# Linear attention and an MLP-mixer: how twenty-four units get the column maximum of k on all partitions

## The chip, the cores and the metric

One NeuronCore of a Trainium2 chip. Its engines are named as the profile names them: PE (TensorE matmuls; PEld are its weight loads), DVE (VectorE), ACT (ScalarE), POOL (GpSimd) and SP (SyncE, which here only issues loads). The metric is the device time of one execution in microseconds, the median of several runs. A profiled execution has a time of its own and a span, from the first to the last recorded instruction.

## The reference

```python
k_s = k - np.max(k, axis=2, keepdims=True)      # over the sequence, per (batch, head, column)
k_s = np.exp(k_s)
k_s = k_s / (np.sum(k_s, axis=2, keepdims=True) + 1e-09)
kv = np.einsum('bhsd,bhse->bhde', k_s, v)
attn = np.einsum('bhsd,bhde->bhse', q_s, kv)    # q_s: softmax of q over its 64 columns
# then, on x = attn as (batch, 576, 512):
h = np.maximum(x.transpose(0, 2, 1) @ w_tok1, 0.0) @ w_tok2
u = x + h.transpose(0, 2, 1)
out = u + np.maximum(u @ w_ch1, 0.0) @ w_ch2
```

q, k and v are float32 of shape (8, 8, 576, 64); the four weights are 64-bit (576x256, 256x576, 512x1536, 1536x512). The softmax of k runs over the sequence, so its maximum is one number for each of the 64 columns of a head.

## The kernel before, in words

**Units.** A unit is one batch and two heads, 32 in all (`NU`). The first eight (`NE`) are "early", the other twenty-four "late". A unit has k twice: `kt_t` with the columns of two heads on the 128 partitions and the sequence along the free dimension, where DVE takes the maximum in one reduction (`mc`, one number per partition, L219), and, for late units, `k_t` with the sequence on the partitions, which the later matmul (`stage_kv`, L277) needs. In `k_t` the maximum must be subtracted along the free dimension, so every partition needs all 128 numbers. Early units take the exponential in `kt_t` and transpose it on PE. A late unit does this: ACT scales an identity with `mc` into a diagonal `dg` (L233), PE multiplies an all-ones matrix with it (L235), which puts the row of 128 maxima on every partition, ACT copies it out of PSUM into `mb` (L236), POOL subtracts `mb` from `k_t` (L237), ACT takes the exponential (L238). `dg` and `mb` have one buffer each, `mc` two, `kt_t` one in the late units, `k_t` and `q_t` two.

**The rest of a unit.** `softmax_q` on DVE and ACT (with ten small exponentials, L251, in four units of each kind); q is split into a high and a low part (`qh` on ACT, `ql` on POOL, L114 and L115) and transposed in 32x32 blocks (L315, L323, `qth`, `qtl`). PE then makes `stage_kv`, `stage_y` (L337), `stage_h1` (L345) and `stage_u` (L381). The result `u` is split into `uh` and `ul` (L388, L389).

**The MLP.** The rows of the result are taken in nine groups of 512. For each group and each of twelve slices `f`, `ch1` makes 12 matmuls (L409), ACT and DVE make `h2h` and `h2l` of them (L412, L413), and `ch2` makes 12 more into four PSUM banks (L421). There are 108 such steps. Products run in float32r with high and low parts.

**Weights.** Each 64-bit weight tile is loaded into a staging buffer (`stg`, L166) and turned into float32 by DVE, ACT, and DVE again (L174 to L181; L181 is the last to read the buffer), and split into `cw` (L114 on ACT, L115 on DVE). Slices 4 to 11 are loaded during the first steps, the last of them through two staging buffers.

**What sets the order.** The kernel is written unit by unit and step by step; a scheduler then lists the instructions of each engine by its own estimates of durations. Each engine runs its list strictly in order, and SP issues its loads in order too, waiting ahead of each until the buffer is free. `soft(n + 1)`, which holds the lines above, is written right behind the first stage of unit n, `begin(n + 2)`, which loads a unit, half a step later.

Of the kernel before, what the change touches and what calls it, by code (L numbers as in the profile page):

```python
# [8 lines left out]
F32 = mybir.dt.float32  # L9
F32R = mybir.dt.float32r  # L10
U32 = mybir.dt.uint32
AF = mybir.ActivationFunctionType
# [3 lines left out]
P = 128  # L16
# [4 lines left out]
def attn_mixer_kernel(ctx: ExitStack, tc: tile.TileContext, q, k, kt, v, wt, out, dims):  # L21
# [3 lines left out]
    nc = tc.nc  # L25
# [10 lines left out]
    NE = 2 * NJ  # L36
# [13 lines left out]
    ident = const.tile([P, P], F32R, name="ident")  # L50
# [11 lines left out]
    ones = const.tile([P, P], F32, name="ones")  # L62
# [26 lines left out]
    dg = lay.tile([P, P], F32, name="dg")  # L89
    for i in range(3):  # L90
        slots[i][1] = lay.tile([P, NJ, CW], F32R, name=f"ul{i}")
    mb = lay.tile([P, P], F32, name="mb")
# [16 lines left out]
    def f32(ap):  # L109
        return ap.bitcast(F32)  # L110
# [8 lines left out]
    def ps_unit(dtype=F32):  # L119

        pools = unit_banks[0]
        pool, name = pools[turn[0] % len(pools)]
        turn[0] += 1
        return pool.tile([P, 512], dtype, name=name)
# [88 lines left out]

    turned_k = []

    def softmax_k(u):
        ktt = u["kt"]
        mc = sm.tile([P, 1], F32, name="mc")
        nc.vector.tensor_reduce(mc, ktt, axis=AX.X, op=ALU.max)  # L219
        kx = u["k"]  # L220
        if u["early"]:
            nc.vector.tensor_scalar(mc, mc, -1.0, None, op0=ALU.mult)
            nc.scalar.activation(ktt, ktt, AF.Exp, bias=mc)
            t = ps_unit()
            for c in range(C):
                nc.tensor.transpose(t[:, c * P : (c + 1) * P], ktt[:, c * P : (c + 1) * P], f32(ident))
            nc.scalar.copy(kx[:, 0:C, :], t.rearrange("p (c d) -> p c d", c=C))
            t = ps_unit()
            turned_k.append(nc.tensor.transpose(t[:, 0:P], ktt[:, S0 : S0 + P], f32(ident)).ins)
            nc.scalar.copy(kx[:, C, :], t[:, 0:P])  # L230
            return

        nc.scalar.activation(dg, f32(ident), AF.Copy, scale=mc)  # L233
        t = ps_unit()
        nc.tensor.matmul(t[:, 0:P], ones, dg, start=True, stop=True)  # L235
        nc.scalar.copy(mb, t[:, 0:P])  # L236
        nc.gpsimd.tensor_tensor(kx, kx, mb.unsqueeze(1).broadcast_to([P, C1, P]), op=ALU.subtract)  # L237
        nc.scalar.activation(kx, kx, AF.Exp)  # L238

# [223 lines left out]
    def soft(n):  # L463
        if n < NU:
            softmax_k(units[n])
            softmax_q(units[n])
# [194 lines left out]
```

## Time and profile before

| | |
|---|---|
| median of 3 runs | 822.23 us (821.69 to 822.65) |
| the profiled execution | 822.09 us, span 820.3 us, 11946 instructions |
| granted TensorE clock | 0.995 of full |
| moved by DMA | 63.55 MB, mean 77 GB/s |

The page of the profile lists the busy time of each engine, then the costliest groups of instructions by line. Matmuls are pipelined, so their busy times overlap and are no cost each; the distance between starts is. "Idle before, <-releaser" is the time that an engine waited ahead of an instruction and what ended that wait. The chain of waits goes back from the last instruction to what released it, step by step.

### The profile page before, as it was taken

What the parts mean: (1) busy time and instruction counts of PE and PEld (TensorE: products, weight loads), DVE (VectorE), ACT (ScalarE), POOL (GpSimd) and SP (SyncE); (2) the same over time, 40 slices, a digit from 0 to 9 for tenths busy, and PEclk for the clock granted to TensorE, in tenths of its full rate; (3) what the DMA queues carried; (4) which work ended last, traced back from release to release, by engine and by line L of the source; (5) the groups of instructions that cost most, each with busy time, mean ns of one, the idle gap of its engine ahead of it and who ended that gap; (6) DMA issues with size and microseconds to landing.
All of it is one profiled execution on the core that took longest, in us unless ns stands there. A gap on an engine that the chain in (4) does not pass through costs nothing.

```text
span 820.3 us, 11946 instructions
## 1 busy us (share of the span) xinstructions
PE 803.5 (98%) x4512; PEld 678.1 (83%) x4512; DVE 490.5 (60%) x1104; ACT 340.0 (41%) x898; POOL 84.4 (10%) x69
## 2 busy tenths in 40 slices
PE   7899999989999999999999999999999999999997
PEld 6688888878888888888888888888888888888886
DVE  6999998897875455855576555845575324113112
ACT  6976564457544344443434443434443421101110
POOL 1000010102201011111111111101111100000100
PEclk9999999999999999999999999999999999999999
DMA  9753433424222112312232221312121001001001
GB/s 298 241 161 93 150 108 113 139 83 126 64 73 85 48 53 63 109 52 64 64 114 63 64 64 35 113 47 63 39 91 48 15 1 51 1 1 51 1 1 51
DMA packets 60634, 63.55 MB, mean 77 GB/s; under 512 B 40865, under 2 KB 40993, under 8 KB 60577
## 3 DMA queue, kind: packets, MB, share of 16 engines
q1 hardware_dynamic: 55392, 53.36, 22.2%
q10 hardware_dynamic: 5184, 9.44, 3.1%
q8 instruction: 35, 0.57, 0.3%
q14 instruction: 23, 0.18, 0.1%
HBM read 53.35 MB, written 9.44 MB: 77 GB/s over the span
## 4 chain that ended last, share of the span: by engine, by line
PE 89%; DVE 6%; DMA 3%; ACT 1%; SPq 1%; issue 0%; DVEq 0%; ACTq 0%
PE ps_h L409 34%; PE ps_o L421 34%; PE ps_h L381 8%; PE ps_h L337 5%; PE ps_h L277 2%; DMA stg<-in_w 2%; PE ps_h L345 1%; DMA kt_t<-in_kt 1%; PE ps_o L381 1%; PE ps_h L235 1%; PE ps_o L337 1%; DVE mc L219 1%; DVE q_t L323 1%; DVE cv_s L176 1%; DVE cv_s L181 1%; DVE stg L179 0%
## 5 line engine op out<-in xcount | busy, mean ns | idle before, releaser
L409 PE MATMUL ps_h<-uh,cw 128*128 128x512 f32 x864 | 268.6, 391 | 0.3 <-DVE cw L115 0.3
L421 PE MATMUL ps_o<-h2h,cw 128*128 128x512 f32 x864 | 250.0, 392 | 2.2 <-DVE cw L115 2.2
L421 PEld LDWEIGHTS ps_o<-h2h,cw 128*128 128x128 f32 x864 | 160.0, 188 | 34.7 <-ACT h2h L412 2.4
L409 PEld LDWEIGHTS ps_h<-uh,cw 128*128 128x128 f32 x864 | 159.3, 188 | 31.6 <-DVE cw L115 0.8
L413 DVE SCALAR_TENSOR_TENSOR h2l<-ps_h,h2h 128x512 fp32r<-128x512 f32 x108 | 74.3, 688 | 170.4 <-ACT h2h L412 170.2
L412 ACT ACTIVATE h2h<-ps_h 128x512 fp32r<-128x512 f32 x108 | 64.4, 596 | 253.8 <-PE ps_h L409 251.5
L409 PE MATMUL ps_h<-ul,cw 128*128 128x512 f32 x432 | 168.7, 390 | 0.0
L421 PE MATMUL ps_o<-h2l,cw 128*128 128x512 f32 x432 | 151.9, 394 | 0.0
L409 PEld LDWEIGHTS ps_h<-ul,cw 128*128 128x128 f32 x432 | 81.1, 188 | 17.4
L421 PEld LDWEIGHTS ps_o<-h2l,cw 128*128 128x128 f32 x432 | 79.7, 188 | 15.9
L323 DVE COPY q_t<-cv_s 32x160 f32<-32x160 f32 (+1 forms) x264 | 62.1, 235 | 45.2 <-POOL ql L115 41.9
L237 POOL TENSOR_TENSOR k_t<-k_t,mb 128x640 f32<-128x640 f32 x24 | 38.0, 1583 | 350.6 <-ACT mb L236 350.6
L115 POOL TENSOR_TENSOR ql<-q_t,qh 128x640 fp32r<-128x640 f32 x24 | 39.2, 1633 | 220.7 <-ACT qh L114 218.2
L245 DVE TENSOR_REDUCE st<-q_t 128x10 f32<-128x640 f32 x32 | 26.2, 817 | 38.2 <-DMA q_t<-in_q 38.2
L323 ACT COPY q_t<-cv_s 32x128 f32<-32x128 f32 (+1 forms) x120 | 36.8, 307 | 2.1 <-DVE cv_s L315 0.7
L256 ACT ACTIVATE q_t<-q_t 128x640 f32<-128x640 f32 x24 | 17.7, 739 | 40.4 <-DVE q_t L255 40.4
L381 PE MATMUL ps_h<-w2h,hh 128*128 128x256 f32 (+1 forms) x112 | 32.6, 299 | 0.0
L381 PE MATMUL ps_h<-w2l,hh 128*128 128x256 f32 (+1 forms) x112 | 32.6, 296 | 0.0
L389 DVE TENSOR_TENSOR ul<-ps_h,uh 128x320 fp32r<-128x320 f32 (+4 forms) x76 | 26.8, 372 | 7.4 <-ACT uh L388 6.8
L388 ACT CAST uh<-ps_h 128x320 fp32r<-128x320 f32 (+4 forms) x76 | 24.4, 337 | 15.6 <-PE ps_h L381 11.2
L381 PE MATMUL ps_h<-w2h,hl 128*128 128x320 f32 (+1 forms) x112 | 29.8, 300 | 0.3 <-DVE hl L353 0.2
L219 DVE TENSOR_REDUCE mc<-kt_t 128x1 f32<-128x640 f32 x32 | 25.9, 809 | 4.8 <-DMA kt_t<-in_kt 3.5
(144 smaller groups left out, 1077.8 us busy)
## 6 DMA issues: line engine op xcount, KB each, us to landing
stg<-in_w SPq DMA_DIRECT2D x28, 512.0 KB, 4.0
kt_t<-in_kt SPq DMA_DIRECT2D x32, 320.0 KB, 3.2
q_t<-in_q SPq DMA_DIRECT2D x32, 320.0 KB, 3.1
v_t<-in_v SPq DMA_DIRECT2D x64, 128.0 KB, 2.6
out<-stg ACTq DMA_DIRECT2D x32, 256.0 KB, 2.1
k_t<-in_k SPq DMA_DIRECT2D x24, 320.0 KB, 3.3
v_t<-in_v SPq DMA_DIRECT2D x32, 32.0 KB, 2.5
out<-part ACTq DMA_DIRECT2D x4, 256.0 KB, 2.3
```

The costliest lines, as they stand in the source:

```text
L115: lo_eng.tensor_tensor(lo, src, f32(hi), op=ALU.subtract)
L219: nc.vector.tensor_reduce(mc, ktt, axis=AX.X, op=ALU.max)
L237: nc.gpsimd.tensor_tensor(kx, kx, mb.unsqueeze(1).broadcast_to([P, C1, P]), op=ALU.subtract)
L245: nc.vector.tensor_reduce(st[:, 0, :], qt, axis=AX.X, op=ALU.max)
L323: eng(qx[ys, 0:n, xs], turned[xs, 0:n, ys])
L337: nc.tensor.matmul(y[:, 0:TOK], a, w, start=(i == 0), stop=(i == len(mm) - 1))
L381: nc.tensor.matmul(t[:, 0:N], a, w, start=(i == 0), stop=(i == len(mm) - 1))
L389: nc.vector.tensor_tensor(ul, src, f32(uh), op=ALU.subtract).ins,
L409: nc.tensor.matmul(t, cw[f][x][:, n, :], w, start=(i == 0), stop=(i == 3 * NJ - 1))
L412: nc.scalar.activation(hh, t, AF.Relu).ins,
L413: nc.vector.scalar_tensor_tensor(hl, t, 0.0, f32(hh), op0=ALU.max, op1=ALU.subtract).ins,
L421: nc.tensor.matmul(o, cw[f][x][:, n, :], w, start=(first and i == 0), stop=(last and i == 2))
```

## The change

For the late units the diagonal, the product with the ones and the copy are not made. Instead SP writes the 128 numbers of `mc` into a row in memory (128 partitions of one number each into 128 numbers that lie together) and reads this row back into `mb`, the same row for each of the 128 partitions. A late unit has its own row, 24 in all. Nothing else is written differently; `dg` stays allocated.

```diff
+    THROUGH = NE
+    dram = ctx.enter_context(tc.tile_pool(name="dram", bufs=2, space=bass.MemoryType.DRAM))
 
     def softmax_k(u):
...
-        nc.scalar.activation(dg, f32(ident), AF.Copy, scale=mc)
-        t = ps_unit()
-        nc.tensor.matmul(t[:, 0:P], ones, dg, start=True, stop=True)
-        nc.scalar.copy(mb, t[:, 0:P])
+        if u["n"] < THROUGH:
+            nc.scalar.activation(dg, f32(ident), AF.Copy, scale=mc)
+            t = ps_unit()
+            nc.tensor.matmul(t[:, 0:P], ones, dg, start=True, stop=True)
+            nc.scalar.copy(mb, t[:, 0:P])
+        else:
+            row = dram.tile([1, P], F32, name="row")
+            nc.sync.dma_start(row.rearrange("o p -> p o"), mc)
+            nc.sync.dma_start(mb, row.broadcast_to([P, P]))
         nc.gpsimd.tensor_tensor(kx, kx, mb.unsqueeze(1).broadcast_to([P, C1, P]), op=ALU.subtract)
         nc.scalar.activation(kx, kx, AF.Exp)
```

`THROUGH` is 8, the number of early units, which return ahead of these lines; so no unit makes the product. Lines behind the change have numbers that are higher by 4 and then by 9.

The scheduler makes new lists of the instructions. Three places.

First, DVE in the loop that turns the last weights into float32. L174 is the first and L181 the last instruction that reads a staging buffer, L115 the split into `cw`, L413 (L422 in the changed kernel) makes `h2l`, and L219 (L223) is the maximum of k. Before:

```order
L177 TENSOR_SCALAR stg<-stg 128x512
L413 SCALAR_TENSOR_TENSOR h2l_112<-ps_h,h2h_108 128x512
L219 TENSOR_REDUCE mc<-kt_t 128x1
L179 SCALAR_TENSOR_TENSOR stg<-stg 128x512
L174 TENSOR_SCALAR cv_s<-stg 128x512
L181 TENSOR_TENSOR cv_s<-stg,cv_s 128x512
L176 SCALAR_TENSOR_TENSOR cv_s<-stg,cv_s 128x512
L115 TENSOR_TENSOR cw_1388<-cv_s,cw_1388 128x4x128
L177 TENSOR_SCALAR stg<-stg 128x512
```

The changed kernel, between the 13th and the 15th `h2l`:

```order
L181 TENSOR_TENSOR cv_s<-stg,cv_s 128x512
L223 TENSOR_REDUCE mc<-kt_t 128x1
L422 SCALAR_TENSOR_TENSOR h2l_113<-ps_h,h2h_109 128x512
L176 SCALAR_TENSOR_TENSOR cv_s<-stg,cv_s 128x512
L115 TENSOR_TENSOR cw_1390<-cv_s,cw_1390 128x4x128
L177 TENSOR_SCALAR stg<-stg 128x512
L174 TENSOR_SCALAR cv_s<-stg 128x512
L179 SCALAR_TENSOR_TENSOR stg<-stg 128x512
L223 TENSOR_REDUCE mc<-kt_t 128x1
L181 TENSOR_TENSOR cv_s<-stg,cv_s 128x512
L176 SCALAR_TENSOR_TENSOR cv_s<-stg,cv_s 128x512
```

Before, the maximum shown is the only one between the 11th `h2l` and the 29th L181; now there are five, two of them in the rows shown. Ahead of the next-to-last split of weights (the last tile that `ch1` needs) stand 21 maxima instead of 13, and by the 23rd `h2l` all 32 stand instead of 16. L174 and the next L181 are also further apart.

Second, PE where the second group's last step is due: the last matmuls of `stage_y` of the first late unit (L337, now L346) and what follows. L421 (L430) is `ch2`, L409 (L418) `ch1`, L345 (L354) is `stage_h1` and L381 (L390) `stage_u`. Before:

```order
L337 MATMUL ps_h<-w1tl,qh 128x256
L421 MATMUL ps_o<-h2h_109,cw_1388 128x512 x8
L421 MATMUL ps_o<-h2l_113,cw_1388 128x512 x4
L345 MATMUL ps_h<-kvf_110,ys 128x128 x2
L381 MATMUL ps_h<-qth,kvh 128x320
L381 MATMUL ps_h<-qtl,kvh 128x320
```

The changed kernel:

```order
L346 MATMUL ps_h<-w1tl,qh 128x256
L354 MATMUL ps_h<-kvf_110,ys 128x128 x2
L390 MATMUL ps_h<-qth,kvh 128x320
L418 MATMUL ps_h<-uh_100,cw_1095 128x512 x2
L418 MATMUL ps_h<-ul_104,cw_1095 128x512
L418 MATMUL ps_h<-uh_100,cw_1095 128x512 x2
```

The `ch2` group, which needs the last weights, moved behind `stage_h1`, a whole `ch1` group and half of `stage_u`. From the 23rd `ch1` group on, PE's order is the same as before but for the products.

Third, SP. Before, a late unit's loads:

```order
L137 DMA kt_t<-in_kt 128x640
L140 DMA q_t<-in_q 128x640
L154 DMA v_t<-in_v 128x4x64 x2
L155 DMA v_t<-in_v 64x2x64
L144 DMA k_t<-in_k 128x640
L137 DMA kt_t<-in_kt 128x640
```

The changed kernel, near the end of the weights loop (L244 writes a row, L245 reads it back):

```order
L244 DMA row<-mc 128x1
L137 DMA kt_t<-in_kt 128x640
L244 DMA row<-mc 128x1
L166 DMA stg<-in_w 128x1024
L137 DMA kt_t<-in_kt 128x640
L154 DMA v_t<-in_v 128x4x64 x2
L155 DMA v_t<-in_v 64x2x64
L144 DMA k_t<-in_k 128x640
```

and in a late unit:

```order
L245 DMA mb<-row 128x128
L140 DMA q_t<-in_q 128x640
L154 DMA v_t<-in_v 128x4x64 x2
L155 DMA v_t<-in_v 64x2x64
L144 DMA k_t<-in_k 128x640
L245 DMA mb<-row 128x128
```

The kt loads and the rows' writes moved out of the late units and stand between the weight loads (L166) and the first late units' loads, where each write waits for its maximum. In a late unit only the row's read is left, behind the load of k of the unit before.

## The prediction

> **What bounds the kernel now.** I read the page's totals first, then busy time by stretches, then the idle times of PE in the one stretch that has any, then the chain of waits there, and last the rows of the instructions that go. The page's totals, and the chain's shares:
>
> ```profile
> PE 803.5 (98%) x4512; PEld 678.1 (83%) x4512; DVE 490.5 (60%) x1104; ACT 340.0 (41%) x898; POOL 84.4 (10%) x69
> PE 89%; DVE 6%; DMA 3%; ACT 1%; SPq 1%; issue 0%; DVEq 0%; ACTq 0%
> ```
>
> Busy time by stretches (busy us per engine, granted clock, DMA share, GB/s):
>
> ```profile
> 100.00:120.00 20.00, 20.00 (x90) 16.56 (x89) 19.69 (x40) 14.06 (x53) 3.08 (x1) 1.00 0.34 113
> 120.00:140.00 20.00, 20.00 (x90) 16.54 (x89) 17.64 (x33) 7.29 (x12) 0.00 (x0) 1.00 0.32 105
> 140.00:160.00 20.00, 20.00 (x108) 16.40 (x106) 16.94 (x31) 8.47 (x16) 1.86 (x1) 1.00 0.43 131
> 160.00:180.00 20.00, 17.48 (x88) 14.55 (x87) 18.29 (x43) 10.22 (x26) 3.14 (x2) 1.00 0.23 69
> 180.00:200.00 20.00, 19.45 (x137) 16.52 (x137) 15.53 (x41) 15.24 (x64) 3.12 (x2) 1.00 0.37 112
> 200.00:240.00 40.00, 40.00 (x244) 34.28 (x243) 30.94 (x71) 20.14 (x48) 6.29 (x4) 1.00 0.24 69
> 360.00:400.00 40.00, 40.00 (x236) 33.91 (x235) 22.44 (x56) 16.77 (x41) 5.97 (x4) 1.00 0.20 51
> ```
>
> From 200 us on PE never pauses and the clock is whole, so there every product taken away is time won. From 100 to 160 PE does not pause either, but VectorE (DVE) is busy 54.3 of 60 us: it turns the last weights from 64-bit pieces into float32. At 160 to 200 PE idles 3.07 us. PE's rows with idle time there, and the chain through the weights (start, length):
>
> ```profile
> 164.35 0.73 PE L409 MATMUL ps_h<-uh,cw 128*128 128x512 f32 x2 [0.34 <-DVE cw L115]
> 171.23 2.09 PE L421 MATMUL ps_o<-h2h,cw 128*128 128x512 f32 x8 [2.18 <-DVE cw L115]
> 183.29 0.49 PE L235 MATMUL ps_h<-dg,ones 128*128 128x128 f32 x2 [0.43 <-DVE h2l L413]
> ...
> 136.73 0.60 DVE cv_s L181
> 137.36 3.24 DMA stg<-in_w
> 141.05 0.61 DVE cv_s L181
> 148.39 0.73 DVE mc L219
> 150.11 0.61 DVE cv_s L181
> 150.74 4.20 DMA stg<-in_w
> 155.39 0.61 DVE cv_s L181
> ```
>
> All three pauses, 2.95 us together, wait for DVE, and the chain behind them is a loop: L181 frees a staging buffer, the next weights load into it (3.24 us), DVE converts them. Two limits, then: PE over most of the span, DVE with the weight loads from about 135 to 185 us.
>
> **What goes.** 24 products of `ones` with the diagonal, their two ACT instructions, and one PSUM bank per unit. Their rows, by form:
>
> ```profile
> L235 PE MATMUL ps_h<-dg,ones 128*128 128x128 f32 x48 | 11.4, 319 | 0.4 <-DVE h2l L413 0.4
> L233 ACT ACTIVATE dg<-ident,mc 128x128 f32<-128x128 f32 x24 | 9.7, 405 | 0.2
> L236 ACT COPY mb<-ps_h 128x128 f32<-128x128 f32 x24 | 6.1, 253 | 5.0 <-PE ps_h L235 5.0
> ```
>
> A product is two matmuls. Their 11.4 us of busy time is no price, because matmuls overlap; the price is by how much the starts after it move. PE around one product, and a long run of 512-column matmuls from the chain:
>
> ```profile
> 200.09 0.38 PE L235 MATMUL ps_h<-dg,ones 128*128 128x128 f32 x2
> 200.23 1.17 PE L421 MATMUL ps_o<-h2l,cw 128*128 128x512 f32 x4
> 201.24 0.62 PE L409 MATMUL ps_h<-uh,cw 128*128 128x512 f32 x2
> ...
> 380.92 5.49 PE ps_o L421 x24
> 396.37 0.42 PE ps_h L235 x2
> ```
>
> The steady pace is 5.49/24 = 0.229 us. From 200.09 to 200.23 the product holds the start back by 0.14 us, and the four matmuls behind it take 1.01 us instead of 4 x 0.229 = 0.915. Together 0.235 us, say 0.23. Bounds: 0.14 (the starts alone) and 0.42 (the chain's piece). 24 x 0.23 = 5.5 us, between 3.4 and 10.1. ACT loses 9.7 + 6.1 us of work; I credit nothing, since ACT is busy 41%.
>
> **What is added.** Per unit a write of 128 numbers from `mc` to memory and a read of the row on all 128 partitions, both on SP. No row shows such transfers; the nearest rows are the smallest loads, 32 KB, then those of kt and k, and one issue on SP:
>
> ```profile
> v_t<-in_v SPq DMA_DIRECT2D x32, 32.0 KB, 2.5
> kt_t<-in_kt SPq DMA_DIRECT2D x32, 320.0 KB, 3.2
> k_t<-in_k SPq DMA_DIRECT2D x24, 320.0 KB, 3.3
> 149.14 0.33 SPq L137 DMA_DIRECT2D kt_t<-in_kt  x1
> ```
>
> So about 2.5 us each and 5.0 for the pair (0.33 us of SP for each issue), against some 0.9 us for diagonal, product and copy. Below: nothing, where hidden; above: the 3.2 us of kt each, 6.4 for the pair. The Trainium skill says the opposite of a recommendation for this: in "DMA: Bandwidth & Descriptors", section "Rules for kernel authors", small transfers are to be merged because under 64 KB one pays mostly overhead. The 2.5 us for 32 KB against 3.2 us for ten times as much agrees.
>
> Whether the pair shows depends on how early it is issued. In a late unit (rows around 375 us):
>
> ```profile
> 375.83 0.59 SPq L144 DMA_DIRECT2D k_t<-in_k  x1
> 376.06 1.58 POOL L237 TENSOR_TENSOR k_t<-k_t,mb 128x640 f32<-128x640 f32 x1 [14.81 <-ACT mb L236]
> 380.95 0.73 ACT L114 CAST qh<-q_t 128x640 fp32r<-128x640 f32 x1 [1.08 <-PE ps_h L337]
> 386.25 0.60 PE L345 MATMUL ps_h<-kvf,ys 128*128 128x128 f32 x4
> ```
>
> In the changed order the writes run many units ahead. The read of `mb` stands on SP right behind the load of k and waits for the subtraction before it; behind it queue the next loads of q, v, k. k lands at about 375.83 + 3.3 = 379.1 us, the subtraction ends at 380.7, then the read starts for a subtraction one period, 22 us, later. Its 2.5 us are hidden, at the upper bound too. ACT's exponential of k now follows at 380.7 to 381.4 and delays `qh` and `ys` by some 0.5 us; PE wants `ys` only at 386.25. Late stage: nothing lost.
>
> **What moves.** Nothing ties the maxima to PE any more. Before, `mc` had to wait for the diagonal and so for a product; now only kt's single buffer and the row's write hold them, and the order runs them ahead of their units. Where DVE's maxima lie now, and the rows of three operations that matter below:
>
> ```profile
> L219 DVE TENSOR_REDUCE mc<-kt_t x32: 762/810/821, 3.7 to 576.9; 128x1 f32<-128x640 f32 x32
> L260 DVE TENSOR_TENSOR q_t<-q_t,st 128x640 f32<-128x640 f32 x32 | 28.4, 888 | 0.6
> L315 DVE STREAM_TRANSPOSE cv_s<-q_t 128x640 f32<-128x640 f32 x24 | 20.3, 844 | 0.7
> L115 DVE TENSOR_TENSOR kvl<-kvf,kvh 128x128 fp32r<-128x128 f32 x24 | 7.3, 302 | 2.3 <-ACT kvh L114 2.3
> ```
>
> They are spread over 577 us. In the changed order 21 maxima instead of 13 stand on DVE ahead of the split (L115) of the last L409 weights, and all 32 are done by the 23rd `h2l`, where it was 16. A maximum is 0.73 us (chain row above): 8 more are 5.8 us. They can fall into the 5.7 us that DVE idles from 100 to 160 (cost 0) or not at all (cost 5.8). The trace prices one: from 141.05 to 150.11 are two rounds with one maximum, 9.06 us, against 2 x 4.32 (136.73 to 141.05) without: 0.42 us. The round after it, in which kt was being loaded beside the weights (issued 149.14), took 5.28 us and its weight load 4.20: 0.96 more. From the 11th `h2l` to the 29th L181 the new order has five maxima, before one. Four more at 0.42 are 1.7 us, at 1.38 they are 5.5. I take 1.7, because the new order leaves more work between a buffer's release and its next use. PE also arrives 0.5 us earlier (two products less before it), so the pause of 0.34 us becomes 0.34 + 0.5 + 1.7 = 2.5.
>
> The pause of 2.18 us goes: PE's order now puts the next L409 group (12 x 0.229 = 2.7 us) and the first late unit's products ahead of the L421 group that waited, more than the 2.18 us that it waited.
>
> Then DVE runs late behind PE: from there to the 18th `h2l` three more maxima, 2.2 us, with no slack (PE waited 0.43 for `h2l` already): 2.6 us of pause.
>
> Last, kt has one buffer, so a maximum cannot start before write issue, kt issue and landing, 0.33 + 0.33 + 3.2 = 3.9 us after the one before. Between the 25th and the 26th DVE has L260, L315 and kvl, 0.89 + 0.84 + 0.30 = 2.0 us; before the 29th, 30th and 31st some 3.3 us each. That makes waits of 1.9 + 3 x 0.6 = 3.7 us inside DVE's order. From 200 to 240 DVE idles 9 us, so I let a third through, 1.2 us (0 to 3.7).
>
> Pauses: 2.5 + 2.6 + 1.2 = 6.3 us instead of 2.95, a loss of 3.4 us. Sum: 3.4 - 5.5 = -2.1 us. The profiled execution took 822.09 us (span 820.3, 1.8 around it), 0.14 below the median of 822.23; so 822.09 - 2.1 = 820.0 us.
>
> **The rivals.** (1) The maxima fall into DVE's idle time: no new pause, -5.5 us, 816.6 us; with the old pauses gone too, 813.6. For it: 5.7 us idle against 5.8; the scheduler places such work where it thinks DVE free. Against it: the 0.42 us above. (2) Slower: the loads of kt. Each maximum pulls a kt load in between the weight loads, and each DVE wait for kt holds up the conversions behind it. At 1.38 us for each of the four maxima (3.8 more than I take) and all 3.7 us of kt's waits (2.5 more) the loss is 3.4 + 6.3 = 9.7 us: 826.3 us. It decides once the new pauses pass 5.5 + 2.95 = 8.5 us. For it: the 4.20 us load; against it: it happened in one round. (3) The skill's rule about small transfers, as a mechanism here: the pair is not hidden, and each of some 20 late units waits for its `mb`. With the 5 us pair on the path in place of 0.9 that is 20 x 4.1 = 82 us; it speaks against it that the read is issued a period ahead. A slip of 0.5 us per unit alone gives 830 us. That the rule (the page named above) fits the 2.5 us row does not make it decide. (4) The products were free, hidden by weight loads: +3.4 us, 825.5 us; the starts at 200.23 and 201.24 speak against it.
>
> **Chances.** My sum 0.50, rival 1 0.22, rival 2 0.18, rival 3 0.05, rival 4 0.05. What a measurement of this kernel can tell from no change is 0.2%, 1.6 us: faster means under 820.6, slower above 823.9. My sum's own range is 818 to 822: 0.28 of it faster, 0.22 the same. Rival 1 is faster (0.22), rival 2 slower but for 0.04, rivals 3 and 4 slower but for 0.02. So faster 0.50, same 0.28, slower 0.22. Range for 8 in 10: from inside rival 1 at 815.5 to inside rival 2 at 825.5 us.
>
> **What would show it.** Right: no L235; matmul starts at 0.229 us across its old place; PE busy 40.00 of 40 from 240 on; pauses of PE for DVE between 155 and 235 us that sum to 5 to 8 us; DVE waits for kt before a few maxima; the 32nd maximum by 235 us instead of 577. Wrong: pauses under 3 us (rival 1) or over 8.5 (rival 2), POOL waiting for the row's read while PE waits for k after 240 us (rival 3), late units that take as long as before (rival 4).

## The result, and the profile after

The changed kernel takes 973.2 us (median of six runs, 971.39 to 977.09) against 822.0 us before (820.6 to 823.94): a ratio of 1.1845, 95% interval 1.1814 to 1.1876. The forecast was 820.0 us with 815.5 to 825.5, so it was wrong by 153 us, in the direction of its second rival and far beyond it. The profiled execution took 972.45 us with a span of 970.6, which is 150.3 us more span than before.

The page's totals and the shares of the chain after, by engine:

```profile
PE 843.9 (87%) x4464; PEld 700.9 (72%) x4464; DVE 490.9 (51%) x1104; ACT 328.1 (34%) x850; POOL 85.6 (9%) x69
PE 59%; DMA 26%; DVE 11%; SPq 1%; issue 1%; ACT 1%; DVEq 0%; ACTq 0%
```

The 48 matmuls are gone (4464 instead of 4512), yet PE is busy 40.4 us longer, and it idles 970.6 - 843.9 = 126.7 us where it idled 16.8. So 109.9 us of the 150.3 are new pauses, and 40.4 are the remaining matmuls taking longer. An estimate from PE's busy time and the granted clock in each stretch between 100 and 400 us gives 37 us for the lower clock, nearly all of it. Transfers were 3% of the chain and are 26%. Busy time by stretches says where (length, then busy us of PE, PEld, DVE, ACT, POOL, then clock, DMA share, GB/s):

```profile
100.00:120.00 20.00, 18.16 (x79) 14.68 (x79) 11.05 (x24) 10.65 (x48) 1.56 (x1) 0.98 0.36 104
140.00:160.00 20.00, 11.12 (x37) 8.29 (x37) 10.04 (x17) 4.07 (x7) 0.00 (x0) 0.84 0.79 75
180.00:200.00 20.00, 9.42 (x23) 7.19 (x24) 9.17 (x16) 3.55 (x6) 0.00 (x0) 0.60 0.63 73
200.00:240.00 40.00, 19.34 (x70) 13.78 (x69) 14.10 (x26) 6.23 (x12) 0.00 (x0) 0.73 0.73 68
280.00:320.00 40.00, 19.89 (x88) 15.59 (x87) 15.98 (x42) 11.16 (x42) 3.09 (x2) 0.71 0.69 94
440.00:480.00 40.00, 40.00 (x225) 34.32 (x224) 19.88 (x51) 15.77 (x37) 6.27 (x4) 1.00 0.18 47
```

Nearly all of it is lost between 100 and 400 us (108 of the 109.9 us of pauses). Neither PE nor DVE is full there: between 180 and 200 us both work less than half of the time, and PE's clock is down to 0.60. The DMA engines meanwhile are busy 0.46 to 0.79 of the time from 140 to 400 us (0.20 to 0.43 before), and that is not because they move more: from 140 to 160 us it is 75 GB/s, where it was 131. From 440 us on PE is full again. The transfers themselves, median time from issue to landing at the end of each row, then the waits that grew, with total, times and longest, and the same two waits before:

```profile
stg<-in_w SPq DMA_DIRECT2D x28, 512.0 KB, 6.3
kt_t<-in_kt SPq DMA_DIRECT2D x32, 320.0 KB, 10.4
mb<-row SPq DMA_DIRECT2D x24, 64.0 KB, 2.9
row<-mc SPq DMA_DIRECT2D x24, 0.5 KB, 8.3
...
DVE mc L223 <- DMA kt_t<-in_kt: 104.5, 22, 9.3
DVE cv_s L174 <- DMA stg<-in_w: 36.0, 7, 8.6
...
DVE mc L219 <- DMA kt_t<-in_kt: 3.5, 4, 1.8
DVE cv_s L174 <- DMA stg<-in_w: 5.2, 5, 2.1
```

The smallest transfer of the kernel, 512 bytes, takes 8.3 us; the read of the same row takes 2.9. And kt's load, which nobody touched, went from 3.2 to 10.4 us. The chain through two maxima shows how they meet (start, length, what):

```profile
155.95 0.83 DVE mc L223
...
156.80 0.33 SPq L244
...
157.22 11.37 DMA kt_t<-in_kt
...
168.69 0.83 DVE mc L223
```

A maximum, its row's write (L244), the next load into kt's one buffer (L137) issued 0.4 us behind it, and 11.37 us until that load is there for the next maximum: 12.74 us from one maximum to the next. DVE works in order, and the weight conversions and `h2l` between two maxima are soon done: its row for the later maximum (idle time before it, and for what, at the end) is

```profile
168.69 0.82 DVE L223 TENSOR_REDUCE mc<-kt_t 128x1 f32<-128x640 f32 x1 [8.72 <-DMA kt_t<-in_kt]
L223 DVE TENSOR_REDUCE mc<-kt_t x32: 802/820/821, 3.8 to 378.5; 128x1 f32<-128x640 f32 x32
```

The last maximum runs at 378.5 us, and a little behind it PE comes free. In the late units, in contrast, what was forecast happened. The chain before, and after, at the first step of a unit and of the one behind it:

```profile
386.41 0.44 PE ps_h L345 x4
...
408.53 0.44 PE ps_h L345 x4
```

```profile
605.25 0.45 PE ps_h L354 x4
...
627.15 0.44 PE ps_h L354 x4
```

22.12 us became 21.90. The other units on both chains agree: 22.03 became 21.84, and the longest 23.05 became 22.8.

### The profile page after: what moved, and what is told of

It reads as the page before. It is cut to its first block, busy times and chain, and to the rows that moved or that the text cites. A ratio compares the mean times of both kernels' runs of the same rounds, so it can differ in the third digit from the quotient of the medians.

```text
span 970.6 us, 11910 instructions
## 1 busy us (share of the span) xinstructions
PE 843.9 (87%) x4464; PEld 700.9 (72%) x4464; DVE 490.9 (51%) x1104; ACT 328.1 (34%) x850; POOL 85.6 (9%) x69
## 4 chain that ended last, share of the span: by engine, by line
PE 59%; DMA 26%; DVE 11%; SPq 1%; issue 1%; ACT 1%; DVEq 0%; ACTq 0%
PE ps_o L430 24%; PE ps_h L418 23%; DMA kt_t<-in_kt 21%; PE ps_h L390 5%; DMA q_t<-in_q 3%; PE ps_h L346 3%; DMA stg<-in_w 2%; DVE mc L223 2%; PE ps_h L286 2%; PE ps_h L354 1%; DVE cv_s L181 1%; DVE stg L179 1%; DVE cv_s L176 1%; DVE ul L398 1%; DVE st L254 1%
## 5 line engine op out<-in xcount | busy, mean ns | idle before, releaser
L418 PE MATMUL ps_h<-uh,cw 128*128 128x512 f32 x864 | 282.2, 408 | 19.4 <-DVE h2l L422 11.1
L430 PE MATMUL ps_o<-h2h,cw 128*128 128x512 f32 x864 | 258.3, 405 | 28.6 <-ACT h2h L421 24.5
L430 PEld LDWEIGHTS ps_o<-h2h,cw 128*128 128x128 f32 x864 | 165.3, 195 | 66.0 <-ACT h2h L421 31.4
L418 PEld LDWEIGHTS ps_h<-uh,cw 128*128 128x128 f32 x864 | 168.9, 199 | 55.1 <-DVE h2l L422 11.7
L430 PE MATMUL ps_o<-h2l,cw 128*128 128x512 f32 x432 | 158.2, 415 | 35.3 <-DVE h2l L422 35.3
L418 PE MATMUL ps_h<-ul,cw 128*128 128x512 f32 x432 | 174.7, 404 | 0.0
L422 DVE SCALAR_TENSOR_TENSOR h2l<-ps_h,h2h 128x512 fp32r<-128x512 f32 x108 | 74.2, 687 | 174.4 <-ACT h2h L421 174.4
L421 ACT ACTIVATE h2h<-ps_h 128x512 fp32r<-128x512 f32 x108 | 64.4, 596 | 246.7 <-PE ps_h L418 246.5
L430 PEld LDWEIGHTS ps_o<-h2l,cw 128*128 128x128 f32 x432 | 83.0, 197 | 56.7 <-DVE h2l L422 39.0
L418 PEld LDWEIGHTS ps_h<-ul,cw 128*128 128x128 f32 x432 | 85.4, 198 | 19.3
L223 DVE TENSOR_REDUCE mc<-kt_t 128x1 f32<-128x640 f32 x32 | 26.1, 817 | 104.7 <-DMA kt_t<-in_kt 104.5
L390 PE MATMUL ps_h<-w2h,hl 128*128 128x320 f32 (+1 forms) x112 | 32.2, 318 | 18.2 <-DVE hl L362 18.2
L115 POOL TENSOR_TENSOR ql<-q_t,qh 128x640 fp32r<-128x640 f32 x24 | 38.7, 1614 | 69.6 <-ACT qh L114 57.6
L247 ACT ACTIVATE k_t<-k_t 128x640 f32<-128x640 f32 x24 | 17.7, 738 | 62.1 <-POOL k_t L246 56.7
L114 ACT CAST cw<-cv_s 128x512 fp32r<-128x512 f32 x24 | 14.8, 616 | 62.0 <-DVE cv_s L181 62.0
L175 ACT ACTIVATE cv_s<-cv_s,ebias 128x512 uint32<-128x512 uint32 (+2 forms) x30 | 20.9, 702 | 42.8 <-DVE cv_s L174 42.5
L390 PEld LDWEIGHTS ps_h<-w2h,hl 128*128 128x128 f32 x112 | 21.4, 202 | 19.1 <-DVE hl L362 19.0
## 6 DMA issues: line engine op xcount, KB each, us to landing
kt_t<-in_kt SPq DMA_DIRECT2D x32, 320.0 KB, 10.4
```

What stands on the lines that cost most here:

```text
L115: lo_eng.tensor_tensor(lo, src, f32(hi), op=ALU.subtract)
L390: nc.tensor.matmul(t[:, 0:N], a, w, start=(i == 0), stop=(i == len(mm) - 1))
L418: nc.tensor.matmul(t, cw[f][x][:, n, :], w, start=(i == 0), stop=(i == 3 * NJ - 1))
L421: nc.scalar.activation(hh, t, AF.Relu).ins,
L422: nc.vector.scalar_tensor_tensor(hl, t, 0.0, f32(hh), op0=ALU.max, op1=ALU.subtract).ins,
L430: nc.tensor.matmul(o, cw[f][x][:, n, :], w, start=(first and i == 0), stop=(last and i == 2))
```

## The experiments

Two theories. **A**: the row's write is slow by its form, 128 numbers of 4 bytes, and loads issued behind it land only after it. **B**: what costs is the order, maxima and kt loads in between the weight loads, whatever the write takes. Eight kernels were run.

**The write by itself.** The kernel before, product kept, with one unused write per late unit from unit 12 on, of four forms in turn:

```diff
+        kind = u["n"] % 4 if u["n"] >= NE + 4 else None
+        if kind == 0:
+            row = dram.tile([1, P], F32, name="row")
+            nc.sync.dma_start(row.rearrange("o p -> p o"), mc)
+        elif kind == 1:
+            wide_row = dram.tile([P, P], F32, name="wide_row")
+            nc.sync.dma_start(wide_row[:, 0:1], mc)
+        elif kind == 2:
+            full_row = dram.tile([P, P], F32, name="full_row")
+            nc.sync.dma_start(full_row, mb)
+        elif kind == 3:
+            short_row = dram.tile([1, P], F32, name="short_row")
+            nc.vector.transpose(dg[:, 0:32], mb[:, 0:32])
+            nc.sync.dma_start(short_row.rearrange("o (b i) -> (o b) i", i=32), dg[0:P:32, 0:32])
```

> The kernel before with its product kept, plus one write to memory per late unit from the twelfth unit on that nothing reads, of four kinds in turn: the maxima as 128 single numbers of 4 B side by side (the change's write), the same 128 numbers 512 B apart, the 64 KB tile as 128 runs of 512 B, and the maxima turned on DVE and written as 4 runs of 128 B. It measures the disputed cost by itself. Theory A (a write of single numbers is slow by its form, and what is queued behind it on SP's queue lands only after it): the first kind 7.5 to 9 us, the second the same if the size of one piece decides and 2.5 to 3.5 us if it is pieces that share a stretch of memory; the third and fourth 2.5 to 3.5 us; loads issued within 1 us of a write of the first kind land 10 us after issue or later. Theory B (the write was slow because kt, stg and q loads crowded the queue; the order of the work is to blame): in this order, where a write comes every 22 us, all four kinds take 2.5 to 3.5 us. Time by both: 820 to 826 us.

One execution took 822.69 us, against 822.36 before. The DMA issues of this kernel (KB each, median us to landing):

```profile
kt_t<-in_kt SPq DMA_DIRECT2D x32, 320.0 KB, 3.5
full_row<-mb SPq DMA_DIRECT2D x5, 64.0 KB, 1.8
row<-mc SPq DMA_DIRECT2D x5, 0.5 KB, 9.3
wide_row<-mc SPq DMA_DIRECT2D x5, 0.5 KB, 1.4
```

Side by side the 128 numbers take 9.3 us in a calm stretch too, so no crowd on the queue is needed, and B's account of the write falls. The same 128 numbers 512 bytes apart take 1.4 us: it is not their size nor their count. A write of 64 KB takes 1.8. The first form is a little above what A expected (7.5 to 9), the second and third well below (2.5 to 3.5). Four kt loads were issued 0.4 to 0.5 us behind a write of the first form: they land 8.1 to 11.6 us after their issue, where kt's median is 3.5, so the cost to the loads shows here too, in three of four as late as A expected (10 us or more). The turned row left no landing time in the trace. Unused, these writes cost nothing that one execution can tell.

**From which distance on.** The same with the numbers 8 to 128 bytes apart, in turn:

```diff
+        kind = (u["n"] - NE) % 5 if u["n"] >= NE + 4 else None
+        if kind == 0:
+            row8 = dram.tile([P, 2], F32, name="row8")
+            nc.sync.dma_start(row8[:, 0:1], mc)
...
+        elif kind == 4:
+            row128 = dram.tile([P, 32], F32, name="row128")
+            nc.sync.dma_start(row128[:, 0:1], mc)
```

> The kernel before with its product kept and one unused write of the 128 maxima per late unit from the twelfth on, the numbers 8, 16, 32, 64 and 128 B apart in turn. At 4 B apart it took 9.3 us and at 512 B 1.4 us. If what is slow is that several pieces fall into one stretch of memory and are written one after the other, the time from issue to landing falls with the pitch, about in proportion to the pieces in a stretch, and is 1.4 to 2 us once each piece has its own; the pitch at which it ends is the size of the stretch (64 B is the guess). If it is something of the packed row alone (its being one piece of 512 B), 8 B apart is already under 3 us.

The source lines of the writes (8, 16, 32, 64, 128 bytes apart, in this order, four of each; times are min/median/max):

```profile
DMA to landing us min/median/max: 3.7/3.9/4.6
DMA to landing us min/median/max: 1.4/2.9/3.6
DMA to landing us min/median/max: 2.0/2.5/2.8
DMA to landing us min/median/max: 1.4/2.5/2.7
DMA to landing us min/median/max: 1.4/2.2/2.5
```

The time falls with the distance, but not in proportion (9.3, 3.9, 2.9, 2.5, 2.5, 2.2, and 1.4 at 512), and 64 bytes is no edge. Both guesses in the expectation are too simple: the distance between the pieces decides, and it has no sharp edge here. The largest step, from 9.3 to 3.9 us, is from pieces that touch to pieces with a gap. One execution took 824.88 us.

**One write instead of 24.** The order stays, with the maxima ahead, and every late unit reads the first one's row, so 23 units subtract another unit's maxima:

```diff
-            row = dram.tile([1, P], F32, name="row")
-            nc.sync.dma_start(row.rearrange("o p -> p o"), mc)
+            if u["n"] == NE:
+                rows_of.append(dram.tile([1, P], F32, name="row"))
+                nc.sync.dma_start(rows_of[0].rearrange("o p -> p o"), mc)
+            row = rows_of[0]
```

> The change with the row of the first late unit alone written; every late unit reads that one row, so 23 of the 24 writes are left out and those units subtract another unit's maxima. Reads, the missing products and maxima ahead of their units stay. Theory A (the write and the loads held behind it cost the time): a maximum's cycle on kt's one buffer falls from 12.7 us to about 4 us (0.83 for the maximum and 3.2 for the load), DVE waits for kt under 20 us in all instead of 104.5, kt's median landing is under 4.5 us, and the time is 815 to 830 us. Theory B (the maxima and kt loads among the weight loads cost it, whatever the write takes): 900 us or more, DVE still waiting for kt 60 us or more.

836.35 us, ratio 1.017 (1.0145 to 1.0196). kt's landing is back at 3.2 us:

```profile
DVE mc L224 <- DMA kt_t<-in_kt: 8.5, 7, 4.0
L224 DVE TENSOR_REDUCE mc<-kt_t x32: 771/814/822, 3.7 to 216.8; 128x1 f32<-128x640 f32 x32
```

So 137 of the 151 us go with 23 writes, and all maxima are done by 217 us, as forecast (235). A's waits hold (8.5 us for kt, where it said under 20), its time does not: 836.35 is 6 us above its upper end of 830. Part of those are the one write that is left, behind which SP stands until 105 us: between 100 and 120 us PE lost 3.07 us (16.93 busy of 20), which it does not lose in the next kernel, whose write is short.

**Another form of the write.** The maxima are turned on DVE and written as 4 runs of 128 bytes; the order stays with the maxima ahead:

```diff
-            nc.sync.dma_start(row.rearrange("o p -> p o"), mc)
+            tr = tr_ring[u["n"] % 2]
+            nc.vector.transpose(tr, mc_ring[u["n"] % 2])
+            nc.sync.dma_start(row.rearrange("o (b i) -> (o b) i", i=32), tr[0:P:32, :])
```

> The change with its write in another form: the maxima are turned by a 32x32 transpose on DVE and written as 4 runs of 128 B; the order of maxima ahead of their units stays as in the change. Theory A: the write lands in 2.5 to 3.5 us, kt's median landing under 5 us, and the time is 815 to 832 us. Theory B: 900 us or more. If it is the wait of later loads for any write to memory, whatever its form, kt stays above 8 us and the time near 970 us.

826.03 us, ratio 1.0043 (1.0029 to 1.0058): theory A again. This kernel is close to what the prediction had in mind, a quick write in the changed order, but for 24 transposes of 0.2 us on DVE, and it is still slower than before. Its stretches:

```profile
140.00:160.00 20.00, 17.80 (x77) 13.89 (x76) 18.12 (x37) 6.96 (x11) 0.00 (x0) 1.00 0.58 184
160.00:180.00 20.00, 14.59 (x76) 11.39 (x75) 18.59 (x42) 9.15 (x19) 2.23 (x2) 0.83 0.48 142
180.00:200.00 20.00, 19.71 (x122) 16.81 (x121) 19.59 (x49) 11.40 (x43) 4.26 (x3) 1.00 0.58 172
200.00:240.00 40.00, 39.05 (x240) 33.55 (x239) 32.09 (x81) 23.64 (x70) 6.49 (x4) 1.00 0.28 79
```

DVE is nearly full again from 160 to 200 us, and PE pauses 2.20 + 5.41 + 0.29 + 0.95 = 8.85 us between 140 and 240 us, against 3.07 before, with the clock at 0.83 around the largest pause.

**Another order.** The slow write stays, but each late unit's maximum is tied on DVE behind an instruction of the unit three before it (`rs`, in its `stage_kv`), so it stands about where it stood before the change. Only late units have this `rs` on the list, so the tie begins with unit 11:

```diff
+        ahead = rs_of.get(u["n"] - 3)
+        with behind([ahead] if ahead is not None else []):
+            nc.vector.tensor_reduce(mc, ktt, axis=AX.X, op=ALU.max)
...
+        got = nc.vector.tensor_scalar(rs, kv[:, D : D + 1], 1e-9, None, op0=ALU.add)
+        if not u["early"]:
+            rs_of[u["n"]] = got.ins
```

> The change with its slow write, but the maximum of a late unit is held on DVE behind the end of the unit three before it, so that maxima stand in DVE's order about where they stood before the change (15 instead of 6 h2l instructions ahead of the twelfth, 72 instead of 22 ahead of the last). Theory A: writes still take about 8 us, but one comes every 22 us and nothing waits for it: no pause of PE from 240 us on, 24 x 0.23 us saved, 814 to 820 us. Theory B: the same time, since the order is undone. If the late stage had no room for the pair of transfers (the third rival of the prediction), PE would pause in it and the time would be 825 us or more.

832.25 us (four executions, 828.32 to 835.1), ratio 1.0123 (1.008 to 1.0166): 141 us better than the change, and 12 us above the upper end of what was expected. The writes take 8.0 us and the kt loads, each issued right behind one, 7.5. From 240 us on this hurts nothing (PE 40.00 of 40 in each stretch), but between 100 and 200 us PE pauses 9.82 us. The chain there (start, length, what):

```profile
106.57 11.08 DMA row<-mc
...
117.70 4.30 DMA mb<-row
...
122.16 2.15 POOL k_t L249
...
124.98 0.71 ACT cv_s L175
```

For the first late units the pair isn't issued a period ahead. SP stands at the read until the row has landed, 11.08 us, the weight loads queued behind it on SP wait too, and then POOL and ACT, whose order has the subtraction and the exponential ahead of a weight conversion (L175). That is the third rival's mechanism, in the one place where nothing covers it.

**Both edits.** The short write and the hold together:

> Both edits together: the maxima turned on DVE and written as 4 runs of 128 B, and each late unit's maximum held on DVE behind the end of the unit three before it. Theory A (the write's form costs through what stands behind it on SP's queue, and the maxima ahead of their units cost a few us beside it): neither is left, PE's pauses from 100 to 240 us come down to between 3 and 5 us (3.07 before the change, 10.5 with the hold and the slow write, 8.8 with the short write alone), the 24 products are saved at 0.22 to 0.23 us each, 5.4 us, and the time is 816 to 820 us, faster than before by 0.3 to 0.7%. If transfers of any form cost the weights stage that much, the pauses stay at 8 us or more and the time is 822 us or more.

819.34 us against 822.14 before, ratio 0.9963 (0.9949 to 0.9977): **faster than the kernel before by 0.4%**. kt lands in 4.1 us, and the pauses from 100 to 240 us are

```profile
160.00:180.00 20.00, 17.18 (x82) 14.45 (x80) 17.34 (x42) 12.12 (x43) 3.13 (x2) 0.91 0.22 61
180.00:200.00 20.00, 18.70 (x126) 15.55 (x127) 16.82 (x44) 12.62 (x43) 3.58 (x2) 1.00 0.38 120
200.00:240.00 40.00, 40.00 (x238) 34.47 (x235) 30.82 (x70) 18.53 (x43) 6.79 (x4) 1.00 0.28 77
```

2.82 + 1.30 = 4.12 us, inside the 3 to 5 expected. PE's busy time fell by 6.3 us (803.46 to 797.18) and its idle time grew by 3.6, of which 1.05 are here and 1.9 in the first 100 us. What those 1.9 are is open; the two kernels with unused writes, which change nothing there, have 1.0 us more idle time in it as well.

The four kernels make a table of two by two (medians, us; the kernel before took 822.0 to 822.4 beside them):

| | maxima ahead, as in the change | maxima held |
|---|---|---|
| 128 single numbers | 973.2 | 832.25 |
| 4 runs of 128 bytes | 826.03 | 819.34 |

Against the kernel with both edits, the slow write alone costs 12.9 us, the order alone 6.7, both together 153.9. Neither A nor B by itself: 134 of the 154 us come only where a slow write meets maxima that run ahead of their units. That they meet in kt's one buffer is read from the chain above; a kernel with two buffers for kt was not run.

**Late units alone.** The slow write stays, but only from unit 16 on, with the hold; units 8 to 15 keep their product:

```diff
-    THROUGH = NE
+    THROUGH = NE + 8
```

> The change, slow write and all, from the sixteenth late-stage product's place on: the units 8 to 15, whose maxima fall among the weight loads, keep their product; units 16 to 31 take the two transfers, their maxima held behind the end of the unit three before. Theory A: the 150 us come wholly from the stretch with weight loads, and a slow write in the late stage is hidden; 16 x 0.22 = 3.5 us are saved and nothing is lost: 817.5 to 820 us, faster by about 0.4%. If a slow write costs a late unit anything through the loads behind it (0.2 us a unit would be enough), the time is 822 us or more.

823.37 us, ratio 1.0015 (1.0002 to 1.0028): no gain. The weights stretch is as before, and late units behind the first few take 21.91 us on the chain here too (from 473.00 to 494.91, the starts of two units' L435 groups). Most of the 3.5 us went at the seam, in one place:

```profile
288.19 1.57 POOL L249 TENSOR_TENSOR k_t<-k_t,mb 128x640 f32<-128x640 f32 x1 [16.08 <-ACT mb L244]
296.41 1.55 POOL L249 TENSOR_TENSOR k_t<-k_t,mb 128x640 f32<-128x640 f32 x1 [6.65 <-DMA mb<-row]
...
PE ps_h L359 <- ACT ys L353: 2.4, 1, 2.4
```

The first read of a row waits for `mb`, which the last unit with a product still reads until 289.76, and then takes 6.5 us behind the next unit's write. POOL waits 6.65 us for it ahead of `ql`, and PE 2.4 us for `ys`; the clock is 0.70 from 300 to 305 us, some 1.5 us more by an estimate from it. So the expectation that nothing is lost was wrong for one unit, and for the others it held.

**Another queue.** The write issued on ACT's queue:

```diff
-            nc.sync.dma_start(row.rearrange("o p -> p o"), mc)
+            nc.scalar.dma_start(row.rearrange("o p -> p o"), mc)
```

> The change with the row's write issued on ACT's queue; the read of it, and all loads, stay on SP's. The write's form and the order of the maxima stay. Theory A1 (loads land late because they stand behind the write's 128 pieces on one and the same queue): kt's median landing falls from 10.4 us to under 5 us, DVE waits for kt under 40 us instead of 104.5, and the time falls to between 826 and 870 us, what is left being the read on SP that holds up the loads behind it until the row has landed, and the maxima among the weight loads. Theory A2 (the engines that move data are themselves held by such a write, whichever queue it came by): kt stays at 8 us or more and the time above 930 us.

968.53 us, ratio 1.1777 (1.176 to 1.1794): A2. The queue makes next to no difference; DVE waits for kt 134.9 us, where it was 104.5. First the landings, then the two hardware queues (q1 is SP's, q10 ACT's: packets, MB, share of 16 engines' time), here and in the kernel with both edits, where no write is slow:

```profile
kt_t<-in_kt SPq DMA_DIRECT2D x32, 320.0 KB, 8.7
row<-mc ACTq DMA_DIRECT2D x24, 0.5 KB, 9.7
q1 hardware_dynamic: 58848, 54.93, 26.3%
q10 hardware_dynamic: 8640, 9.45, 3.0%
```

```profile
q1 hardware_dynamic: 59040, 54.95, 22.5%
q10 hardware_dynamic: 5184, 9.44, 3.0%
```

26.3% of 16 x 967.5 us is 4071 us of engine time; 22.5% of 16 x 817.6 is 2943. SP's packets, with no write of a row among them, take 1.1 ms of engine time longer for the same bytes. ACT's queue, which carries the rows here, took 3.0% of 16 x 967.5 = 464 us; in the change, where it carries none, 2.9% of 16 x 970.6 = 450 us. So the rows' own packets hold the engines little; it is the loads beside them that take long. The records of single packets in the change say the same: all packets of 4 bytes on SP's queue, the rows' among them, took 65 us together, but kt's, q's and k's packets of 2560 bytes took 2810 us, where the same packets took 1508 before; 418 of them took over 1 us, and before none.

## Why the prediction was wrong

- **The step that failed: "about 2.5 us each and 5.0 for the pair".** The read was right (2.9 us). The write was not: 8.3 us, outside the bounds as well, whose upper end was kt's 3.2 us. Those bounds came from loads, all of them transfers with long runs, and the write's row is of another kind: 128 pieces of 4 bytes side by side. No row of the trace before showed one, and the honest bound from above was open.
- **What hung on it: "0.33 + 0.33 + 3.2 = 3.9 us after the one before".** The cycle through kt's one buffer was named, with its place, and it is what set the time. But its 3.2 us took the load as not touched by the write just ahead. It took 11.37, the cycle 12.7, and with 22 maxima waiting the 3.7 us of waits inside DVE became 104.5. The step treated two transfers issued 0.4 us apart as independent.
- **The load's wait for the write is not one of queue order.** The kernel with the write on ACT's queue shows that: around 150 to 200 us write and load are issued within 0.01 us of each other, on two queues, and the load takes 8.6 to 9.6 us. The Trainium skill says so, in "DMA: Bandwidth & Descriptors", section "Queues, rings and completion order": the queues of SP and ACT are rings on the same 16 engines, and the write that reports a transfer's end lands only after every earlier write of its engine, "across its queues". The held kernel agrees: of a kt load issued at 320.63 us, 0.46 us behind a row's write, the last packet ends at 324.63, but the load counts as landed at 328.31, just behind the row at 328.15. In the change there is more to it. The row written at 156.80 has landed at 165.51, yet packets of the kt load issued at 157.22 run until 168.30, one of them for 8.9 us, where their median is 0.10. There the data themselves are late, and why is open.
- **"What moves", 3.4 us.** Undersized on its own account. With a short write in the same order the pauses are 8.85 us between 140 and 240 us, where I had 6.3, and the time is 826.03. Rival 2, priced at 826.3, has the time of that kernel and the place: kt's loads are a third of its chain from 140 to 182 us, and DVE is nearly full. That the time fits so well is partly luck. Rival 2 is a sum with 12.6 us of pauses and 5.5 us saved; measured are 8.85, and a busy time of PE that fell by only 4.0 us, at a clock of 0.83 around the largest pause; and DVE's waits for kt are 5.7 us in all, where they were 3.5. The added transposes lie in the same stretch, and their share isn't told apart, so that the forecast would have been on the wrong side without the slow write too is likely, not shown. My sentence "the new order leaves more work between a buffer's release and its next use" is where the smaller price was chosen, and no row carried it.
- **"24 x 0.23 = 5.5 us": right.** 0.22 us per late unit on the chain (22.12 to 21.90), and 6.3 us less busy time of PE where the clock is nearly whole throughout. Rival 4, free products, is out.
- **"Late stage: nothing lost": right, with one limit.** PE has no pause from 440 us on in the change, and none from 240 us on in the held kernel, where each slow write falls into a late unit. The limit is the first unit that uses a row, in the held kernel and where only units 16 and up have it: there the read isn't a period ahead, and the pair's time shows. Rival 3 was placed in all late units and belongs in the first.
- **The clock was not in the sum at all.** A pause was priced by its length. In the change, 40.4 us were lost beside the 109.9 us of pauses, by the estimate above nearly all by matmuls that ran at 0.60 to 0.86 of the clock where PE paused; in the short-write kernel 0.83 in the stretch of the largest pause. That the pauses cause the lower clock wasn't tested by itself; the lower clocks stand in stretches with pauses or right behind one (0.91 from 120 to 140 us in the kernel with one write, where PE is full again), but not every pause has one (1.00 from 140 to 160 us with the short write, beside 2.20 us of pauses). The Trainium skill describes it, in "TensorE: Matmul & The Clock Gate", section "HAM oscillation — how this bites in real kernels": waits for transfers between short bursts of matmuls let the clock be lowered again and again. The stretches agree, 0.60 where PE is busy 9.42 of 20 us.

## What to carry to other kernels

A transfer that the trace doesn't show has no price from rows of another kind: see how its pieces lie in memory, not only how many bytes it has, and measure one such transfer, unused, in the kernel that is there. A slow write is paid by the loads issued right after it, here on SP's queue, whether the write went by SP's or ACT's; it is harmless where those are a period ahead and dear where they refill a single buffer that an in-order engine waits for. When an edit takes away a dependence, the order of the whole program may move; holding the work where it was is a change of a few lines, and here it and a better form of the write turn a loss of 18% into a gain of 0.4%.

## What the runs showed of the hardware

- A write of 128 numbers of 4 bytes from 128 partitions to 512 bytes of memory lands 8 to 10 us after its issue (medians of 8.3, 9.3, 8.0 and 9.7 in four kernels). With the numbers 8 bytes apart it takes 3.9 us, at 512 bytes 1.4. What makes close pieces slow wasn't found.
- The same row as 4 runs of 128 bytes behind a transpose on DVE has no landing in the trace. A bound: the read of the row waits on SP for the write, and from 200 us on it is issued 3.8 us after it at the median (2.0 to 4.7), where it is 8.0 (7.0 to 9.3) with the slow write and the maxima held alike. SP's wait ahead of the read is 2.07 us at the median, where it is 7.02 (the rows of the kernel with both edits and of the held kernel):

```profile
L253 SPq EVENT_SEMAPHORE  x29: 17/2074/3412, 106.8 to 601.2; - x29
```

```profile
L248 SPq EVENT_SEMAPHORE  x26: 17/7016/8257, 110.5 to 608.8; - x26
```

- Loads of 320 KB that take 3.2 us at the median land 8 to 12 us after issue when such a write was issued just before them on their queue (7.7 us in the held kernel, 8.1 to 11.6 in the kernel with unused writes, 11.4 in the change). With the write issued on ACT's queue at the same moment the median is 8.7 us.
